# One attention and feed-forward kernel: bias loads after the first pair's loads, scores before tail transposes, another bank for the tail-tail scores

## The chip, the cores and the metric

The kernel runs on one core of a Trainium2 chip. The metric is device microseconds of one execution; lower is better. The engines are named as in the profile: PE (TensorE, matrix products and transposes), ACT (ScalarE), DVE (VectorE), POOL (GpSimd) and SP (SyncE, which only issues transfers). Each engine takes its instructions in the order in which they stand in its own queue, and an instruction that waits holds up everything behind it on that engine.

## The reference, cut to what matters

```python
B, H, S, D = 8, 8, 576, 64                      # q, k, v: [B, H, S, D]
scores = matmul(q, k^T) / sqrt(D) + bias_table[bucket(|i - j|)]   # one bias per head and distance
attn   = exp(scores - max) / sum
x      = (attn @ v)  as [B*S, H*D] = [4608, 512]
out    = ((x @ w_a) * (x @ w_b)) @ w_out        # w_a, w_b: [512, 1536], w_out: [1536, 512]
```

The kernel takes no maximum; it multiplies exp(scores) by exp(bias) instead of adding the bias, and divides by the sum at the end.

## The kernel before, in words

**Pairs.** The 64 heads of all batches are worked through as 32 pairs of heads, p = 0 to 31, four pairs to a batch. Of the 576 positions 512 are the main part (four tiles of 128) and 64 are the tail. For each pair: `qk1(p, t)` makes the scores of key tile t for both heads into a two-bank PSUM buffer of the pool sc (two buffers), `ex(p, t)` takes the Exp of it on ACT (L353), `mul(p, t)` multiplies the band near the diagonal by exp(bias) on DVE (L361). `qk_tail(p)` makes the scores that touch the tail: main keys with tail queries (qkt, L367), tail keys with main queries (qkt, L370) and tail with tail (qktt, L373, into a bank of its own, `pt`); `ex_tail` is their Exp, the small one of qktt first. `av(p, jq)` multiplies by V for query block jq, and `norm(p, 0)` (blocks 0 to 2) and `norm(p, 3)` (blocks 3 and 4) divide by the sum on DVE into XG. `t_x` transposes XG on PE, and `c_x` copies it out of PSUM into `xn_sb`, the input of the feed-forward part. `av_part` is av of pair 3, cut by key tiles.

**Banks.** Apart from sc there are one bank AV (pool `ps_av`), one bank TR (`ps_tr`) and two banks FF (`ps_ff`). Whoever asks for a bank waits until its last reader is done. Q and K of the first three batches are transposed on PE (`t_q`, `t_k` for pair 4 on, `t32`, `q_next`, `k_next` before that) into such a bank, and copied to QT and KT by `c_q`, `c_k`.

**Start.** The head of the kernel (pairs 0 to 3) is written out by hand. The bias table (32 x 8) and a one-hot matrix (oh) are loaded first, on SP's and ACT's queues, then q and k of pair 0 (one head on each of the two queues), then pair 1 and the tails on SP. PE makes five warm-up products on zeros, the product of table and one-hot (L217), three more warm-ups, and then the transposes of k tile 0, of q, and of k tiles 1 to 3 (`t32`, L581). ACT takes the Exp of the product (L220) and stores it to DRAM (`tab`, L221). From there POOL loads the bias windows W0 to W3, one for each pair of heads (`load_w`, L166), and SP the tail window Wt (L225). POOL's queue is: identity, eight cleared tiles, six loads of q, k, v of pairs 2 and 0, W0, two of vt, W1, four of vm, W2, q and k of pair 4, W3, and then the feed-forward weights. SP's queue behind Wt holds the loads of pair 3 (`load32(3, ...)`).

**Transition.** At the end of batch 0 `t_x(0)` to `t_x(2)` take TR, FF, FF; `t_q(4)` and `t_k(4)` take FF, FF; `t_x(3)` takes AV.

**From pair 4 on** each step s is a list of operations with places U in it. At each U some units of the feed-forward part of an earlier batch are put in; a unit is `ff_a` (four products pa and a copy ha on ACT), `ff_b` (four products pb and the multiplication g on DVE) or a third of an output tile (`ff_o`). A step gets a quota of units (12 in step 4, then 7, 6, 4, 4, and 9 from step 9 on), spread evenly over its nine places, so that with fewer than nine some places stay empty. In steps 5 to 10 the step also transposes q and k of pair s + 1, both through the bank TR; qktt of pair s takes TR as well for p < 12.

Of the kernel before, what the change touches and what calls it, by code (L numbers as in the profile page):

```python
# [13 lines left out]
def kernel(  # L14
# [11 lines left out]
    nc = tc.nc  # L26
# [139 lines left out]
        eng.dma_start(out=W_sb[hp][:, :, :],  # L166
                      in_=bass.AP(tensor=tab, offset=2 * hp * TB, ap=[[1, 128], [TB, 2], [1, 384]]))

    nc.sync.dma_start(out=bt_sb[0:NB, :], in_=bias_table)
    nc.scalar.dma_start(out=oh_sb[0:NB, :], in_=oh_handle.ap())  # L170
    make_identity(nc, id32[:, :])
    def pad(eng, x, n):
        eng.memset(x[0:64, :, 1, 0:n], 0.0)
# [6 lines left out]
    def load32(p, src, out, engs):  # L180
        for h in range(2):
            load_h(engs[h], src, out[:, p, :, h, :], 0, 2 * p + h)

    load32(0, q, q32, (nc.sync, nc.scalar))
    load32(0, k, k32, (nc.sync, nc.scalar))
    load32(1, q, q32, (nc.sync, nc.sync))
    load32(1, k, k32, (nc.sync, nc.sync))

# [21 lines left out]
    def warm_up(n):  # L210
        for _ in range(n):
            nc.tensor.matmul(out=warm[:, :], lhsT=zero_sb[:, 0:128], rhs=zero_sb[:, :],
                             start=True, stop=True)

    warm_up(5)
    tps = ps_av.tile([128, 512], FP32, tag="av", name="tab_ps")
    nc.tensor.matmul(out=tps[0:H, 0:NR], lhsT=bt_sb[0:NB, :], rhs=oh_sb[0:NB, :],  # L217
                     start=True, stop=True)
    warm_up(3)
    nc.scalar.activation(out=tab_sb[0:H, 127:127 + NR], in_=tps[0:H, 0:NR], func=ACTF.Exp)  # L220
    nc.scalar.dma_start(out=tab.ap(), in_=tab_sb[0:H, :])  # L221

# [30 lines left out]
    def copy(eng, out, in_):  # L253
        if eng is nc.scalar:
            nc.scalar.activation(out=out, in_=in_, func=ACTF.Copy)
        else:
            nc.vector.tensor_copy(out=out, in_=in_)  # L257
# [21 lines left out]
    def bank(where, dt, name):  # L279
        return where[0].tile([128, 512 if dt is FP32 else 1024], dt, tag=where[1], name=name)  # L280
# [53 lines left out]
    def qk1(p, t, fill=0):  # L334
        qT = qT_(p)
        ps = ps_sc.tile([128, 2, 512], FP32, tag="sc", name=f"qk{p}_{t}")
        for _ in range(fill):
            nc.tensor.matmul(out=ps[:, 0, :], lhsT=zero_sb[:, 0:128], rhs=zero_sb[:, :],
                             start=True, stop=True)
        for hh in range(2):  # L340
            r = slice(64 * hh, 64 * hh + 64)
            nc.tensor.matmul(out=ps[:, hh, :], lhsT=kT_(p, t)[r, :],  # L342
                             rhs=qT[r, :, :], start=True, stop=True)
        st[p]["ps", t] = ps

    def qk(p, t0):
        qk1(p, t0)
        qk1(p, t0 + 1)

    def ex(p, t):  # L350
        ps = st[p]["ps", t]
        at = atp.tile([128, 2, SM], BF16, tag="at", name=f"at{p}_{t}")
        nc.scalar.activation(out=at[:, :, :], in_=ps[:, :, :], func=ACTF.Exp, scale=scale)  # L353
        st[p]["at", t] = at
# [9 lines left out]
    def qk_tail(p):  # L364
        ps = ps_sc.tile([128, 2, 512], FP32, tag="sc", name=f"qkt{p}")
        for t in range(NM):
            nc.tensor.matmul(  # L367
                out=ps[:, 0, :].rearrange("p (h t c) -> p h t c", h=2, t=NM)[:, :, t, :],
                lhsT=kT_(p, t), rhs=qTt_(p), start=True, stop=True)
        nc.tensor.matmul(out=ps[:, 1, :], lhsT=kTt_(p), rhs=qT_(p), start=True, stop=True)  # L370
        pt = bank(TR if p < R3 else AV, FP32, f"qktt{p}")
        for hh in range(2):
            nc.tensor.matmul(out=pt[:, 0:ST], lhsT=kTt_(p), rhs=qTt_(p)[:, ST * hh:ST * hh + ST],  # L373
                             start=(hh == 0), stop=(hh == 1))
        st[p]["ps"] = (ps, pt)
# [204 lines left out]
    def t32(ps, src, p, t):  # L580
        nc.tensor.transpose(ps[:, 128 * t:128 * t + 128], src[:, p, t, :, :], id32[:, :])  # L581

    psk0, psq0 = bank(FF, FP32, "trk0a"), bank(TR, FP32, "trq0a")
    psq1, psk1 = bank(AV, FP32, "trq0b"), bank(FF, FP32, "trk0b")
    t32(psk0, k32, 0, 0)
    for t in range(NM):
        t32(psq0 if t < 2 else psq1, q32, 0, t)
    copy(ACT, QT[0][:, 0:256], psq0[:, 0:256])
    copy(None, KT[0][:, 0:128], psk0[:, 0:128])
    for t in range(1, NM):  # L590
        t32(psk1, k32, 0, t)
    copy(None, QT[0][:, 256:512], psq1[:, 256:512])
    copy(None, KT[0][:, 128:SM], psk1[:, 128:512])
    qk1(0, 0)
    qk1(0, 1, 1)
# [19 lines left out]
    def tails_next(p0, n, eng):  # L615
        ps = bank(FF, FP32, f"trt{p0}")
        for i in range(2 * n):
            nc.tensor.transpose(ps[:, 128 * i:128 * i + 128],
                                (qt32 if i % 2 else kt32)[:, p0 + i // 2, :, :], id32[:, :])
        for i in range(n):  # L620
            copy(eng, KT[(p0 + i) % 2][:, SM:SM + 256], ps[:, 256 * i:256 * i + 256])
# [9 lines left out]
    load32(3, k, k32, (nc.sync, nc.sync))  # L631
    qk1(0, 3)
    ex(0, 2)
    tails_next(0, 2, None)
    qk1(1, 0)
    ex(0, 3)
    ex(1, 0)
    qk_tail(0)
# [5 lines left out]
    for s in (1, 2):  # L644
        if s > 1:
            ex(s, 0)
        mul(s - 1, 3)
        mul_tail(s - 1)
        q_next(s)
        qk1(s, 2)  # L650
        ex(s, 1)
        k_next(s)
        qk1(s, 3)
        ex(s, 2)
        tails_next(s + 1, 1, ACT)
        qk_tail(s)
        mul(s, 0)
        av(s - 1, 0)
        av(s - 1, 1)
        av(s - 1, 2)  # L660
        norm(s - 1, 0)
        mul(s, 1)
        ex(s, 3)
        av(s - 1, 3, FF)
        qk1(s + 1, 0)
        ex_tail(s)
        av(s - 1, 4)
        norm(s - 1, 3)
        mul(s, 2)
        qk1(s + 1, 1)  # L670
# [18 lines left out]
    ex(3, 2)  # L689
    av(2, 3, FF)  # L690
    av(2, 4)
    c_x(1)
    norm(2, 3)
    ex_tail(3)
    qk1(3, 3)
# [2 lines left out]
    t_x(2, FF)  # L698
    mul(3, 1)
    av_part(3, 0)  # L700
    c_x(2, ACT)
    t_q(4, FF)
    c_q(4, ACT)
# [12 lines left out]
    t_x(3, AV, range(3))  # L716
    t_x(3, AV, range(3, 5))
    ff_mm(0, 0, wb_sb, "pb", 0, 3)
    c_x(3)

    def tails4():
        ps = bank(TR, BF16, "trt4")
# [15 lines left out]
    for s in range(4, NP + 1):  # L738
        new = s < NP
        U = "unit"  # L740
        A = lambda *jq: (lambda: [av(s - 1, j, AV if j < 3 or s >= R3 else TR) for j in jq])
        N = lambda j: (lambda: norm(s - 1, j))
        steps = []
        if s == R3:
            ring3 = True
        if s == 4:
            steps += [U, U, lambda: qk1(4, 0), lambda: ex(4, 0), lambda: qk1(4, 1), U, lambda: ex(4, 1),
                      lambda: qk1(4, 2), U, lambda: ex(4, 2), lambda: qk1(4, 3), lambda: ex(4, 3),
                      lambda: mul(4, 0), U, tails4, U, lambda: qk_tail(4), lambda: ex_tail(4),
                      lambda: mul(4, 1), U, lambda: mul(4, 2), U, lambda: mul(4, 3),  # L750
                      lambda: mul_tail(4), U, lambda: t_q(5, TR), lambda: c_q(5), U,
                      lambda: t_k(5, TR), lambda: c_k(5), U, U]
        elif new:
            e = early((s + 1) // 4)
            steps += [lambda: qk(s, 0), lambda: ex(s, 0), U, lambda: ex(s, 1), A(0, 1, 2), N(0), U,
                      lambda: mul(s, 0)]
            av34 = [A(3, 4), N(3)]
            if s - 1 in XD:
                av34 += [lambda: t_x(s - 1), lambda: turns(s)]
            if s < R3:  # L760
                steps += av34
            steps += [U, lambda: mul(s, 1)]
            if s >= R3:
                steps += av34
            steps += [lambda: qk(s, 2), lambda: ex(s, 2)]
            if e:
                steps += [lambda: t_q(s + 1, TR), lambda: c_q(s + 1)]
            steps += [U, lambda: ex(s, 3), U, lambda: mul(s, 2)]
            if e:
                steps += [lambda: t_k(s + 1, TR), lambda: c_k(s + 1)]  # L770
            steps += [U, lambda: mul(s, 3), lambda: qk_tail(s), lambda: ex_tail(s), U]
            if s - 1 not in XD:
                steps += [lambda: t_x(s - 1, TR), lambda: c_x(s - 1), lambda: turns(s)]
            steps += [U, lambda: mul_tail(s), U]
        else:
            steps += [A(0, 1, 2), N(0), U, A(3, 4), N(3), U, lambda: t_x(s - 1, AV),
                      lambda: c_x(s - 1), U, U, U, U, U, U, U]
        quota = quotas.get(s, 9)
        seen, put = 0, 0
        nu = sum(1 for x in steps if x is U)  # L780
        for x in steps:
            if x is U:
                seen += 1
                n = (quota * seen + nu - 1) // nu - put
                put_units(n)
                put += n
            else:
                x()
        b = s // 4 + 1
        if new and s % 4 == 2 and b + 1 < B:  # L790
            load_qkt(b + 1)
        if new and 2 <= b < B:
            if s % 4 == 0:
                load_v(b)
                if b % 2 == 0:
                    load_vt(b, 2)
# [31 lines left out]
```

The softmax here doesn't subtract the row's maximum and nothing guards it: scores larger than these inputs give would overflow.

## Time and profile before

| | |
|---|---|
| median of 8 runs | 418.5 us (418.17 to 418.68) |
| profiled execution, its own time | 418.17 us |
| its span, first to last instruction | 416.4 us |
| granted PE clock, mean | 0.999 |
| PE busy | 403.1 us (97%) |
| ACT busy | 245.3 us (59%) |
| DVE busy | 197.3 us (47%) |
| POOL busy | 119.4 us (29%) |

The profile is of one execution. Times in it count from the first instruction. In a line of the timeline the columns are start and length in us, engine, line of the kernel, operation, what is written from what, its shape, how many were merged, and in brackets how long the engine was idle before it and what ended that. Matrix products overlap with the next ones, so the starts of two products say more than the length of one. A line of the chain has start, length and what it is. A line of the waits has the waiting instruction, what it waited for, the us in total, how often, and the longest.

### The profile page before, as it was taken

Reading aid. Unit: us, or ns where it says so; the run is one execution under the profiler, and the core shown is the slowest. Engines: PE = TensorE matmul, PEld = TensorE weight load, DVE = VectorE, ACT = ScalarE, POOL = GpSimd, SP = SyncE. Lnnn points to the kernel's source line nnn. Section 1 sums busy time; section 2 is a strip of 40 time slices with the busy share of each in tenths; the row PEclk is TensorE's granted clock in tenths of the full one; section 3 lists DMA queues with packets and bytes.
Section 4 is the critical chain, followed back from the end, with each engine's and each line's share of the span. In section 5 each row is a group of like instructions: output and inputs, shape, how many; then the busy total and the mean of one; then the engine's idle time right before and its main releaser. Section 6 shows DMA issues by size and latency. Waiting matters only on the chain.

```text
span 416.4 us, 8424 instructions
## 1 busy us (share of the span) xinstructions
PE 403.1 (97%) x3350; PEld 207.5 (50%) x3407; DVE 197.3 (47%) x485; ACT 245.3 (59%) x345; POOL 119.4 (29%) x161
## 2 busy tenths in 40 slices
PE   8799999999999999999999999999999999999996
PEld 3573555555454555544554455555545554444443
DVE  4585666556542555255525553455425540430430
ACT  4887566756656766577666665666567642322321
POOL 9898839904428000920073003000000000000000
PEclk9999999999999999999999999999999999999999
DMA  9999999999949950999099919921120002002004
GB/s 160 191 162 171 159 171 150 177 147 105 124 60 171 177 44 17 169 185 96 16 117 194 120 20 75 174 51 39 41 90 5 12 17 101 2 0 102 2 0 101
DMA packets 164935, 40.75 MB, mean 98 GB/s; under 512 B 155320, under 2 KB 160224, under 8 KB 164896
## 3 DMA queue, kind: packets, MB, share of 16 engines
q0 software_dynamic: 110448, 18.75, 63.2%
q1 hardware_dynamic: 53168, 21.03, 27.7%
q10 hardware_dynamic: 1280, 0.43, 0.5%
q8 instruction: 26, 0.43, 0.4%
q14 instruction: 13, 0.11, 0.1%
HBM read 38.77 MB, written 9.45 MB: 116 GB/s over the span
## 4 chain that ended last, share of the span: by engine, by line
PE 91%; DVE 3%; POOL 2%; issue 1%; DMA 1%; ACT 1%; DVEq 0%; POOLq 0%; ACTq 0%
PE pb L511 22%; PE pa L511 22%; PE po L542 22%; PE av L412 9%; PE qk L342 7%; PE av L403 2%; PE qkt L367 1%; PE qkt L370 1%; DMA W<-bias_tab 1%; DVE at L361 1%; PE qktt L373 1%; PE trx L475 1%; PE po L530 1%; DVE KT L257 1%; DVE XG L449 1%
## 5 line engine op out<-in xcount | busy, mean ns | idle before, releaser
L353 ACT ACTIVATE at<-qk 128x1024 bf16<-128x1024 f32 x128 | 126.2, 1023 | 24.7 <-PE qk L342 24.7
L523 DVE TENSOR_TENSOR g<-pb,ha 128x512 bf16<-128x512 f32 x108 | 74.7, 691 | 118.2 <-PE pb L511 105.1
L511 PE MATMUL pa<-xn,wa 128*128 128x512 bf16 x417 | 110.1, 380 | 1.1 <-issue 0.3
L511 PE MATMUL pb<-xn,wb 128*128 128x512 bf16 x411 | 109.1, 379 | 1.1 <-issue 0.2
L518 ACT ACTIVATE ha<-pa 128x512 f32<-128x512 f32 x108 | 64.6, 598 | 66.7 <-PE pa L511 66.1
L542 PE MATMUL po<-wo,g 128*128 128x512 bf16 x403 | 96.3, 380 | 1.1 <-issue 0.3
L511 PEld LDWEIGHTS <-wa 128*128 128x128 bf16 x432 | 39.3, 98 | 49.7 <-issue 8.8
L361 DVE TENSOR_TENSOR at<-at,W 128x512 bf16<-128x512 bf16 (+1 forms) x128 | 59.0, 483 | 8.4 <-ACT at L353 5.5
L511 PEld LDWEIGHTS <-wb 128*128 128x128 bf16 x432 | 39.4, 98 | 46.8 <-issue 5.9
L542 PEld LDWEIGHTS <-g 128*128 128x128 bf16 x420 | 37.9, 98 | 46.3 <-issue 7.4
L123 POOL DMA_DIRECT2D vm<-in_v_dram x32 | 28.2, 919 | 102.2 <-PE av L412 61.9
L546 ACT ACTIVATE ob<-po 128x512 f32<-128x512 f32 x35 | 20.9, 597 | 60.7 <-PE po L542 58.7
L412 PE MATMUL av<-vm,at 128*128 128x65 bf16 x992 | 43.3, 193 | 0.0
L412 PEld LDWEIGHTS <-at 128*128 128x128 bf16 x992 | 39.4, 97 | 6.2
L448 DVE RECIPROCAL rc<-av 128x6 f32<-128x6 f32 x64 | 12.0, 187 | 53.8 <-PE av L412 52.1
L403 PE MATMUL av<-vt,att 128*128 128x130 bf16 x156 | 34.7, 222 | 0.0
L381 ACT ACTIVATE att<-qkt 128x1024 bf16<-128x1024 f32 x32 | 32.7, 1020 | 0.0
L449 DVE TENSOR_TENSOR XG<-av,rc 128x384 bf16<-128x384 f32 x64 | 31.4, 491 | 2.4 <-DVE rc L448 0.2
L123 POOL DMA_DIRECT2D qn<-in_q_dram x28 | 24.4, 919 | 24.2 <-PE trq L291 16.9
L123 POOL DMA_DIRECT2D kn<-in_k_dram x28 | 24.5, 916 | 4.1 <-DMA vt<-in_v_dram 1.9
L342 PE MATMUL qk<-QTb,KTb 64*128 64x512 bf16 x160 | 24.2, 381 | 0.0
L403 PEld LDWEIGHTS <-att 128*128 128x128 bf16 x156 | 15.3, 98 | 7.4 <-issue 0.7
(121 smaller groups left out, 239.9 us busy)
## 6 DMA issues: line engine op xcount, KB each, us to landing
out_dram<-ob SPq DMA_DIRECT2D x32, 256.0 KB, 4.3
vm<-in_v_dram POOLq DMA_DIRECT2D x28, 128.0 KB, 5.4
qn<-in_q_dram POOLq DMA_DIRECT2D x24, 128.0 KB, 7.8
kn<-in_k_dram POOLq DMA_DIRECT2D x24, 128.0 KB, 9.6
wa<-in_moe_w_a_dram POOLq DMA_DIRECT2D x3, 512.0 KB, 6.8
wb<-in_moe_w_b_dram POOLq DMA_DIRECT2D x3, 512.0 KB, 10.0
wo<-in_moe_w_out_dram POOLq DMA_DIRECT2D x1, 1536.0 KB, 13.1
W<-bias_tab POOLq DMA_DIRECT2D x4, 192.0 KB, 5.5
```

The source lines that it names most:

```text
L123: nc.gpsimd.dma_start(out=(vm[b % 2][:, h0:h1, t, 0:Dh] if dst is None else dst[b % 2][:, :].rearrange("p (t h d) -> p t h d", h=H, t=NM)[ ...
L342: nc.tensor.matmul(out=ps[:, hh, :], lhsT=kT_(p, t)[r, :], rhs=qT[r, :, :], start=True, stop=True)
L353: nc.scalar.activation(out=at[:, :, :], in_=ps[:, :, :], func=ACTF.Exp, scale=scale)
L361: nc.vector.tensor_tensor(out=at[:, :, lo:hi], in0=at[:, :, lo:hi], in1=w[:, :, y:(None if z < 0 else z):-1], op=MULT)
L381: nc.scalar.activation(out=at[:, 0:1024].rearrange("p (a x) -> p a x", a=2), in_=ps[:, :, :], func=ACTF.Exp, scale=scale)
L403: nc.tensor.matmul(out=pav[:, slot, :, :], lhsT=x, rhs=vt[b // 2 % 2][:, 4 * i + hp, :, 0:Dh + 1], start=fresh, stop=True, skip_group_chec ...
L412: nc.tensor.matmul(out=pav[:, slot, hh, :], lhsT=x, rhs=vm[i][:, 2 * hp + hh, t, 0:Dh + 1], start=False, stop=True, skip_group_check=True)
L449: nc.vector.tensor_tensor(out=xg[:, j0:j0 + n, :, :], in0=pav[:, 0:n, :, 0:Dh], in1=rc.unsqueeze(3).to_broadcast([128, n, 2, Dh]), op=MULT)
L511: nc.tensor.matmul(out=ff[key][:, :], lhsT=w[df // FW][:, mc, 128 * (df % FW):128 * (df % FW) + 128], rhs=xn_sb[mc][:, xin(c)], start=(i = ...
L518: nc.scalar.activation(out=ha[:, :], in_=ff["pa"][:, :], func=ACTF.Copy)
L523: nc.vector.tensor_tensor(out=g_sb[df][:, :], in0=ff["pb"][:, :], in1=ff["ha"][:, :], op=MULT)
L542: nc.tensor.matmul(out=po[:, :], lhsT=g_sb[df][:, 128 * tt:128 * tt + 128], rhs=wo_sb[:, df, :], start=(df == 0), stop=(df == NDF - 1))
```

## The change

1. The loads of the bias table and of the one-hot matrix stand behind the loads of q and k of pair 0 on SP's and ACT's queues.
2. Seven warm-ups ahead of the table product and one behind it, instead of five and three. The transposes of pair 0 run q first, then all of k; KT's first 128 columns are copied by ACT instead of DVE.
3. `qk1(1, 0)` stands ahead of `tails_next(0, 2)` on PE.
4. `tails_next(s + 1, 1)` in s = 1, 2 copies on DVE instead of ACT.
5. qktt takes the bank AV instead of TR for pairs 4 to 11.
6. `c_x(1)` moves from DVE (between av and norm of pair 2) to ACT, behind the Exp of pair 3's last tile and just ahead of `c_x(2)`. The copy `c_x(3)` is split: 384 columns on ACT, 128 and the 64 of the tail on DVE.
7. In the steps from pair 5 on, the place U that stood behind `t_q`, `c_q` of the next pair stands ahead of them. PE's order changes by this in steps 5, 6, 9 and 10; in steps 7 and 8 that place is empty.

```diff
-    nc.sync.dma_start(out=bt_sb[0:NB, :], in_=bias_table)
-    nc.scalar.dma_start(out=oh_sb[0:NB, :], in_=oh_handle.ap())
...
     load32(0, q, q32, (nc.sync, nc.scalar))
     load32(0, k, k32, (nc.sync, nc.scalar))
+    nc.sync.dma_start(out=bt_sb[0:NB, :], in_=bias_table)
+    nc.scalar.dma_start(out=oh_sb[0:NB, :], in_=oh_handle.ap())
...
-    warm_up(5)
+    warm_up(7)
     tps = ps_av.tile([128, 512], FP32, tag="av", name="tab_ps")
     nc.tensor.matmul(out=tps[0:H, 0:NR], lhsT=bt_sb[0:NB, :], rhs=oh_sb[0:NB, :],
                      start=True, stop=True)
-    warm_up(3)
+    warm_up(1)
...
-        pt = bank(TR if p < R3 else AV, FP32, f"qktt{p}")
+        pt = bank(TR if p < 4 else AV, FP32, f"qktt{p}")
...
-    t32(psk0, k32, 0, 0)
     for t in range(NM):
         t32(psq0 if t < 2 else psq1, q32, 0, t)
+    for t in range(NM):
+        t32(psk1 if t else psk0, k32, 0, t)
     copy(ACT, QT[0][:, 0:256], psq0[:, 0:256])
-    copy(None, KT[0][:, 0:128], psk0[:, 0:128])
-    for t in range(1, NM):
-        t32(psk1, k32, 0, t)
     copy(None, QT[0][:, 256:512], psq1[:, 256:512])
+    copy(ACT, KT[0][:, 0:128], psk0[:, 0:128])
     copy(None, KT[0][:, 128:SM], psk1[:, 128:512])
...
     ex(0, 2)
+    qk1(1, 0)
     tails_next(0, 2, None)
-    qk1(1, 0)
     ex(0, 3)
...
-        tails_next(s + 1, 1, ACT)
+        tails_next(s + 1, 1, None)
...
     av(2, 4)
-    c_x(1)
     norm(2, 3)
...
     av_part(3, 0)
+    c_x(1, ACT)
     c_x(2, ACT)
...
-    c_x(3)
+    copy(ACT, xn_sb[3][:, 0:384], st[3]["x"][:, 0:384])
+    copy(None, xn_sb[3][:, 384:SM], st[3]["x"][:, 384:SM])
+    copy(None, xn_sb[3][:, xc(0)[1]], st[3]["x"][:, SM:S])
...
-            steps += [lambda: qk(s, 2), lambda: ex(s, 2)]
+            steps += [lambda: qk(s, 2), lambda: ex(s, 2), U]
             if e:
                 steps += [lambda: t_q(s + 1, TR), lambda: c_q(s + 1)]
-            steps += [U, lambda: ex(s, 3), U, lambda: mul(s, 2)]
+            steps += [lambda: ex(s, 3), U, lambda: mul(s, 2)]
```

## The prediction

> **What bounds the kernel now.** I read the page first: TensorE (PE) is busy 403.1 of 416.4 us, so from about 34 us on a microsecond is won only where PE itself waits, and lost wherever a new wait stands in its queue. Then the busy times by stretch, to see where PE isn't full.
>
> ```profile
> 18.00:28.00 10.00, 9.86 (x157) 6.88 (x155) 9.27 (x30) 9.08 (x13) 8.99 (x16) 1.00 1.39 159
> ```
>
> The columns are stretch, length, then busy us of PE, weight loads, VectorE (DVE), ScalarE (ACT), GpSimd (POOL). Between 18 and 28 us DVE (9.27) and ACT (9.08) are nearly full too; from 34 to 104 PE is busy 67.81 of 70, ACT 46.50 and DVE 42.00. Next the chain of waits in the first 36 us:
>
> ```profile
> 8.03 1.42 POOL vm L129 x2
> 9.44 4.81 DMA W<-bias_tab
> ...
> 16.35 0.35 DVE QT L257
> 16.70 0.04 issue
> 16.74 0.22 PE qktt L373 x2
> ```
>
> The chain comes down POOL's queue (qn, kn, vm from 4.95 on, W0's issue at 9.44) and passes through the landing of W0, the first bias window. The multiplications of pair 0 (L361) wait for it; behind them in DVE's queue stands the copy of pair 2's QT, and that frees the bank for pair 1's qktt on PE. The timeline says how each engine stands to it:
>
> ```profile
> 4.90 0.79 ACTq L221 DMA_DIRECT2D bias_tab<-tab_sb  x1
> 6.17 0.38 ACT L255 ACTIVATE QT<-trq0a 128x256 bf16<-128x256 f32 x1 [1.29 <-PE trq0a L581]
> ...
> 12.04 1.02 ACT L353 ACTIVATE at<-qk 128x1024 bf16<-128x1024 f32 x1 [0.97 <-PE qk L342]
> ...
> 14.35 1.70 DVE L361 TENSOR_TENSOR at<-at,W 128x512 bf16<-128x512 bf16 x4 [1.89 <-DMA W<-bias_tab]
> ```
>
> DVE idles 1.89 us for W0, longer than any wait of ACT between 7.3 and 34. Last, PE's waits between 46 and 104 us:
>
> ```profile
> PE qktt L373 <- DVE KT L257: 1.0, 4, 0.4
> PE trq L291 <- DVE XG L449: 0.2, 1, 0.2
> ```
>
> **Part 1, bias loads behind q and k of pair 0.** The one-hot load (oh) goes from first to third on ACT's queue: its issue moves from 0.75 to 0.75+0.54+0.53 = 1.82. If it takes 1.8 us to land as before, it is there at 3.6; if it stays behind k on the same queue, it lands after k, which took 3.6 us from its issue at 1.77 and is now issued 0.48 earlier: 4.9. I take 4.9, because two loads of 128 KB stand before it on its queue and the loads landed in the order of issue (oh 2.58, q 4.09, k 5.40).
>
> *A rule against the change: the Trainium skill, "DMA: Bandwidth & Descriptors", section "Queues, rings and completion order", says that each DMA engine takes a queue's descriptors in ring order. By it oh can't pass k and 4.9 holds; without it 3.6 is open. The landings above agree.*
>
> PE's queue has the table product (L217) ahead of all transposes, in both kernels. It started at 3.44 after the fifth warm-up; now it waits until 4.9, 1.46 later. It is followed by the Exp (4.50 to 4.87) and the store of the table (4.90), whose landing released SyncE's Wt load at 8.64; with 1.46 added that is 10.1. POOL reaches its W0 issue at 9.44 and now waits there until 10.1: 0.66 late, with vt, W1, vm, W2, the weights behind it. (Ends: oh at 3.6 costs nothing, the table landing at 8.8; oh at 5.0 costs 0.8.) Is the 0.66 hidden in the transfer queue? The 128-byte packets of the six loads before W0 have all begun by 11.75, and W0's first packet began at 11.61, 2.17 after its issue, like qn's first (4.90 to 7.00, 2.1). W0 was not queued, so the delay passes. W1 was queued behind vt (6.6 us to landing against 4.8), so a part may be absorbed: 0 to 0.66. DVE starts pair 1 with W1's landing and is then full until 28, so W1's delay is what reaches 28 us. I take **+0.6** (0 to +0.8). On SyncE's queue Wt waits 1.46 longer and the loads of pair 3 behind it go from 10.43 to about 11.6; they landed at 16.9 (q) and 18.6 (k), would land near 18.1 and 19.8, and are read at 19.20 and 20.10: hidden, with 0.3 to spare for k.
>
> **Part 2, first transposes, pair 1's scores early.** The ScalarE queue issues the table's store for 0.79 us. That was hidden (4.90 to 5.69, before QT's copy at 6.17). Now Exp runs 5.96 to 6.33, the issue to 7.15, QT's copy to 7.53, KT's copy (128 columns, new on ACT; between 0.26 for 64 columns and 0.38 for 256) to 7.80, the first score and its 0.43 to the Exp: 8.27 instead of 7.30. Four Exps later pair 1's first stands at 8.27 + 4 x 0.94 = 12.03; in the trace it is at 12.04 after its 0.97 idle, which the reordering removes. So the two cancel. The tails' transposes, which waited for their load until 11.03, now stand behind that score: 11.4 to 11.85, DVE's copy to 12.3, qkt and qktt to 13.0, so ex_tail starts at 13.05 instead of 12.96. The 0.1 is hidden by W0: ACT's ex_tail of pair 1 waits for qktt, and so for W0, anyway.
>
> **Part 3, tail copies from ACT to DVE (pairs 2, 3).** ACT loses 2 x 0.28. DVE gains 2 x 0.34: the first falls in DVE's 0.94 us wait for W1, the second in its 0.35 wait for av at 23.08. At nothing; 0.34 each if that cover goes, and no gain from ACT, which waits for PE again at 27.1 (0.48).
>
> **Part 4, end of batch 0.**
>
> ```profile
> 28.12 1.03 ACT L353 ACTIVATE at<-qk 128x1024 bf16<-128x1024 f32 x1
> 29.02 0.73 ACT L255 ACTIVATE xn<-trx 128x512 bf16<-128x512 bf16 x2
> ...
> 29.06 0.39 PE L291 MATMUL trq<-cst_sb,qn 128*128 128x128 bf16 x4
> ```
>
> c_x(1) leaves DVE, where it ran 27.30 to 27.81 and ended as DVE had to wait for av anyway (0.01 gained), and stands on ACT after ex(3,3). Its bank trx1 is one of two; trx2 takes the other, so t_q(4) on PE now waits for c_x(1): as c_x(2) did, it would end at 29.75, and PE resumes at 29.80 instead of 29.06. Queued behind it: av_part of pair 3, norm, t_x(3), the first feed-forward product. PE is dense there, so **+0.74**; zero only if ACT ran 0.74 ahead of PE, which ex_tail(3) waiting for PE denies. The split of c_x(3) replaces a DVE copy of 0.42 by an ACT copy of 384 columns: between 0.38 (256) and 0.62 (512), 0.50 by proportion, **+0.08**.
>
> **Part 5, qktt in the value bank, unit before t_q.** A step without waiting starts 0.216 after the 512-column product; in pairs 5 to 9 it starts 0.583, 0.589, 0.588, 0.588 and 0.526 after. Together 1.79 lost; the value bank was read long before, so **-1.79**. The moved unit has a price. In pair 5 (7 units for 9 places) nothing is left between t_q and t_k, which share one bank, and the DVE copy between them now stands behind a g multiplication.
>
> ```profile
> 50.86 1.03 PE L511 MATMUL pb<-xn,wb 128*128 128x512 bf16 x4
> 51.06 0.42 DVE L257 COPY QT<-trq 128x512 bf16<-128x512 bf16 x1 [0.23 <-PE trq L291]
> ...
> 51.72 0.39 PE L311 MATMUL trk<-cst_sb,kn 128*128 128x128 bf16 x4
> ...
> 51.99 0.69 DVE L523 TENSOR_TENSOR g<-pb,ha 128x512 bf16<-128x512 f32 x1 [0.51 <-PE pb L511]
> ```
>
> pb moves up 0.23, g starts at 51.76, the QT copy 0.61 later at 52.37 and ends at 52.79; trk at 52.83 instead of 51.72: **+1.11**. Pairs 6 and 10 have one unit between (0.86); the same sum gives a wait of 0.23 each. Pair 6 drops its 0.27 wait for XG (**-0.04**); pair 10 pays **+0.23**. Pair 9's unit before is pa, with no g: nothing; pairs 7, 8 have no unit there.
>
> **Sum.** 0.6 + 0 + 0.74 + 0.08 - 1.79 + 1.11 - 0.04 + 0.23 = +0.93. The profiled execution took 418.17 (span 416.4 and 1.8 around it), the lowest of the eight; the median is 418.5. On it: **419.4**.
>
> **The clock.** The warm-ups stand 0.43 us apart; from 5.64 the 128-column transposes stand 0.11 apart, and the granted clock's record begins at 5.62, after 4.4 us of nearly unbroken work. Now seven warm-ups end at 1.20 + 7 x 0.43 = 4.2 and PE is idle until 4.9. If it stays slow for the eight transposes, that is 0.87 on ACT's start; W0's 0.66 and ACT's 0.28 cover it. If it stays slow until 14, PE's 6.15 busy us of 6 to 14 nearly double: some +2.
>
> *The Trainium skill, "TensorE: Matmul & The Clock Gate", "Part 1: The HAM clock gate", asks for one busy window of about 3.4 us. Seven warm-ups fill 3.0: by the rule the clock would rise later than in the trace and the +2 would be due; no run here shows it yet.*
>
> **Rivals.** (A) W0's delay is absorbed: oh lands early or the transfers catch up. For it: DMA is idle a part of 12 to 14 us (73 to 176 GB/s). Sum 0.33: 418.8. (B) Faster: ACT, not W0, sets the head. Then the 0.28s count and c_x(1) is done before PE asks: 0.08 - 0.49 - 0.56 = -0.97: 417.5. It decides if W0 lands by 14.3 and DVE doesn't wait for it; against it stands the 1.89 idle. (C) The slow clock: +0.93 + 2 = 421.4.
>
> **How the numbers follow.** Forecast 0.55, with 418.6 to 419.8 as its own range (head 0 to 0.8, part 4 0.6 to 0.9); A 0.18, B 0.12, C 0.15. What a measurement can tell from no change is 0.2%, 0.84 us, so the forecast lies just over that: of its 0.55 I give 0.35 to slower and 0.20 to same; of A 0.04 and 0.14. Slower 0.35 + 0.04 + 0.15 = 0.54, same 0.34, faster 0.12. The range leaves out B and the upper part of C: 418.2 to 420.7.
>
> **What would show it.** Right: the table product starts near 4.9, W0's issue near 10.1, DVE's wait for W0 is longer than 1.89; trq of pair 4 waits for ACT's xn copy; no qktt wait after 46 us; one wait of about 1.1 us of trk for the QT copy near 53. Wrong: W0 landing at 14.3 or before, trq of pair 4 not waiting, or transposes 0.21 apart after 6 us.

## The result and the profile after

The changed kernel takes 420.61 us in the median of 11 runs (419.03 to 421.58); the kernel before took 418.48 in the 31 runs beside them (417.9 to 420.13). The ratio is 1.0047 with a 95% interval of 1.0037 to 1.0057: slower by 2.0 us (1.5 to 2.4), where +0.93 was forecast. The profiled execution took 420.32, its span 418.5 against 416.4.

The span says at once where to look. Three places cut it into parts that can be compared between the two traces: the start of the Exp of pair 3's last tile, the start of pair 4's first Exp, and the end of the last instruction.

| part of the span, us | before | after | difference | forecast |
|---|---|---|---|---|
| head, to the last Exp of pair 3 | 28.12 | 29.65 | +1.53 | +0.60 |
| transition, to pair 4's first Exp | 5.83 | 6.78 | +0.95 | +0.82 |
| the rest, to the end | 379.11 | 378.75 | -0.36 | -0.49 |
| sum | 413.06 | 415.18 | +2.12 | +0.93 |

(The span ends some 3.3 us after the last compute instruction in both.) Two of the three parts came out within 0.13 us of the forecast. The head did not. (How far it is off, one profile says only roughly: in the five profiles of kernels whose code is the same up to this Exp, the kernel before and four of the runs below, the head takes between 28.12 and 29.04 us, and the kernel before has the shortest.) Here is the chain of waits of the changed kernel there (start, length, what it was):

```profile
1.90 3.68 DMA oh_sb<-oh
5.62 0.59 PE tab_ps L217 x2
...
7.85 0.61 PE qk L342 x2
8.46 0.54 PE qk L338
9.00 0.54 PE qk L342 x2
9.54 1.05 PE trq L581 x4
...
11.91 0.69 DVE KT L257
12.66 0.39 PE qk L342 x2
13.04 0.60 PE trt L617 x4
13.67 0.43 DVE KT L257
```

Before, this chain came down POOL's queue to W0's landing. Now W0 is not on it. It starts with the landing of the one-hot matrix at 5.58 (forecast 4.9), goes through PE's products, which between 8 and 10.5 us stand 0.54 apart (0.32 in the kernel before), and then through the K copy that pair 1's first scores wait for and the tails' transposes behind them. The wait is in PE's list, one line for each sort of wait (us in total, times, longest):

```profile
PE tab_ps L217 <- DMA oh_sb<-oh: 1.4, 1, 1.4
```

The busy times by stretch show why the products stood so far apart. The columns are as before: PE, weight loads, DVE, ACT, POOL, then PE's granted clock, the DMA share and GB/s.

```profile
4.20:5.70 1.50, 0.11 (x2) 0.08 (x2) 0.00 (x0) 0.00 (x0) 1.46 (x3) 1.00 1.36 209
5.70:7.40 1.70, 1.70 (x11) 0.94 (x10) 0.24 (x1) 0.53 (x2) 1.70 (x4) 0.99 1.24 166
7.40:10.80 3.40, 3.16 (x12) 1.17 (x10) 0.92 (x3) 2.44 (x4) 3.16 (x5) 0.50 1.81 156
```

PE is busy 0.11 of the 1.50 us in which it waits for oh. From 7.4 to 10.8 the clock is at half, 0.50, and PE is then busy 3.16 us for 12 instructions; before, the same stretch had a clock of 1.00 and 16 instructions in 2.58 us:

```profile
7.40:10.80 3.40, 2.58 (x16) 1.19 (x15) 1.39 (x4) 3.40 (x4) 3.40 (x6) 1.00 2.34 160
```

So ACT gets its scores late. First the kernel before, then the changed one:

```profile
7.30 3.77 ACT L353 ACTIVATE at<-qk 128x1024 bf16<-128x1024 f32 x4 [0.75 <-PE qk L342]
...
12.96 0.22 ACT L380 ACTIVATE att<-qktt 128x64 bf16<-128x64 f32 x1
```

```profile
8.50 2.10 ACT L353 ACTIVATE at<-qk 128x1024 bf16<-128x1024 f32 x2 [0.70 <-PE qk L342]
11.32 2.86 ACT L353 ACTIVATE at<-qk 128x1024 bf16<-128x1024 f32 x3 [0.72 <-PE qk L342]
14.86 0.22 ACT L380 ACTIVATE att<-qktt 128x64 bf16<-128x64 f32 x1 [0.68 <-PE qktt L373]
```

The first Exp stands at 8.50 (before 7.30, forecast 8.27), but the Exp of pair 0's tails at 14.86 (before 12.96, forecast 13.05). Most of the half-clock stretch lies between the two.

At the transition, PE's list has the new wait that was forecast, and ACT's and DVE's timelines have one that was not:

```profile
PE trq L291 <- ACT xn L255: 0.4, 1, 0.4
```

```profile
30.55 1.34 ACT L255 ACTIVATE xn<-trx 128x512 bf16<-128x512 bf16 x4
...
34.68 0.49 ACT L255 ACTIVATE xn<-trx 128x384 bf16<-128x384 bf16 x1 [0.83 <-PE trx L475]
```

```profile
35.20 0.32 DVE L257 COPY xn<-trx 128x128 bf16<-128x128 bf16 x2 [0.90 <-ACT xn L255]
```

The ACT part of the split copy `c_x(3)` runs from 34.68 to 35.17, and the DVE part, meant to run beside it, starts at 35.20 and names the ACT copy as what it waited for. Further on, PE's waits between 46 and 106 us are one line, where the kernel before had the four of qktt:

```profile
PE trk L311 <- DVE QT L257: 1.0, 1, 1.0
```

### The profile page after: what moved, and what is told of

Same layout as the page of the kernel before. It is cut to its first block, busy times and chain, and to the rows that moved or that the text cites. A ratio compares the mean times of both kernels' runs of the same rounds, so it can differ in the third digit from the quotient of the medians.

```text
span 418.5 us, 8427 instructions
## 1 busy us (share of the span) xinstructions
PE 403.7 (96%) x3350; PEld 207.8 (50%) x3407; DVE 197.2 (47%) x484; ACT 246.0 (59%) x347; POOL 119.4 (29%) x161
## 4 chain that ended last, share of the span: by engine, by line
PE 93%; ACT 2%; DVE 2%; issue 1%; DMA 1%; ACTq 0%; DVEq 0%
PE pa L511 22%; PE pb L511 22%; PE po L542 22%; PE av L412 9%; PE qk L342 8%; PE av L403 2%; PE qkt L367 2%; PE qkt L370 1%; ACT at L353 1%; DMA oh_sb<-oh 1%; PE po L530 1%; PE trx L475 1%; PE qktt L373 1%; PE trk L311 0%; DVE g L523 0%
```

## The experiments

A ratio stands against runs of the kernel before on the same chip (medians 418.49 to 418.63), with its 95% interval; 0.1% is 0.42 us. Theory 1: the late one-hot load, through PE's queue and the clock, makes the loss of the head. Theory 2, that of the forecast: the bias window W0 is late. Theory 3: the new order of scores and tails does it.

**The bias loads alone.** The kernel before, with

```diff
-    nc.sync.dma_start(out=bt_sb[0:NB, :], in_=bias_table)
-    nc.scalar.dma_start(out=oh_sb[0:NB, :], in_=oh_handle.ap())
...
     load32(0, k, k32, (nc.sync, nc.scalar))
+    nc.sync.dma_start(out=bt_sb[0:NB, :], in_=bias_table)
+    nc.scalar.dma_start(out=oh_sb[0:NB, :], in_=oh_handle.ap())
...
-    warm_up(5)
+    warm_up(7)
...
-    warm_up(3)
+    warm_up(1)
```

> The kernel before with the two bias loads alone put behind the first pair, and the warm-ups 7 and 1. Theory 1 (the table product, ahead of the transposes in PE's queue, waits for oh_sb, and the clock falls to half after that idle stretch): oh_sb lands near 5.6, the first transposes start near 6.3, the clock is at half for one stretch of 3.4 us, the exponential of the tails of pair 0 is 1.0 to 1.6 later than 12.96, and the total is 1.0 to 1.6 us above the kernel before. Theory 2 (the tables W are late, as forecast): the clock stays full after 7 us, W0 lands 0.2 to 0.6 later, the multiplications wait for it, total +0.2 to +0.6. Theory 3 (the order of scores and tails makes the loss): the loads alone cost under 0.3.

Measured: 420.13 us, ratio 1.0030 (1.0017 to 1.0043), so +1.3 (0.7 to 1.8). The table product starts at 5.58, the first transposes at 6.33, the Exp of pair 0's tails at 14.05 (+1.09), and the clock record has half speed from 7.66 to 11.07:

```profile
7.40:10.80 3.40, 3.16 (x13) 1.28 (x12) 0.98 (x3) 2.23 (x3) 2.98 (x5) 0.54 1.90 164
```

```profile
15.24 1.70 DVE L361 TENSOR_TENSOR at<-at,W 128x512 bf16<-128x512 bf16 x4 [1.68 <-ACT att L381]
```

W0 landed at 15.14 here (before 14.26). DVE's multiplications ended their wait at 15.21 with ACT, 0.07 after W0. So theory 1 holds for the total and for where the clock falls, theory 3 is not needed, and theory 2 is not refuted: in this execution both came together. The head of this profile, which is of the fastest of the twelve executions, takes 29.01 us; two profiles further down that load the bias first take 29.04 and 29.01, with W0 landing at 15.17 and 15.15. The loss is seen in the medians, not in this trace.

**The bias loads put back.** The changed kernel with the loads first again and `warm_up(5)`, `warm_up(3)`.

> The changed kernel with the bias loads first again and the warm-ups 5 and 3; all else stays changed. Theory 1: oh_sb lands near 2.6, no half-clock stretch after 7 us, 1.0 to 1.6 us below the changed kernel, so 419.0 to 419.6. Theory 2: 0.2 to 0.6 below it. Theory 3 (order): within 0.3 of the changed kernel.

Measured: 419.14, ratio 1.0011 (1.0002 to 1.0021). Against the changed kernel's 1.0047 that is 1.5 us less, the gain that theory 1 named. The clock is full from 4.99, and the first Exp starts at 6.87, earlier than before the change. But DVE waits longer for W0 than in either kernel:

```profile
15.20 1.70 DVE L361 TENSOR_TENSOR at<-at,W 128x512 bf16<-128x512 bf16 x4 [2.74 <-DMA W<-bias_tab]
```

W0 was issued at 9.44 as in the kernel before and landed at 15.10 instead of 14.26. Theory 3 is out as a cause by itself: all of the new order is still in this kernel. Whether the order adds to late loads was not tried; with the clock falling, the tails' Exp stands at 14.86 with it (the changed kernel) and at 14.05 without it (the bias loads alone).

**More warm-ups.** The changed kernel with

```diff
-    warm_up(7)
+    warm_up(13)
```

> The changed kernel with 13 warm-up products ahead of the table product in place of 7: PE is busy until about 5.6, when oh_sb lands, so nothing real starts later. If the half-clock stretch of 7.4 to 10.8 us comes from the idle stretch before the table product and carries most of the loss: full clock after 4 us, transposes of trq1 0.11 apart in place of 0.21, the exponential of pair 0's tails 0.6 to 1.0 earlier, total 0.6 to 1.0 below the changed kernel. If the late oh_sb alone carries it: 0 to 0.2 below.

Measured: 419.81, ratio 1.0025 (1.0017 to 1.0034): 0.9 us below the changed kernel, though oh lands just as late (5.69) and the first Exp starts at 8.38. The stretch that was at half clock:

```profile
7.40:10.80 3.40, 3.11 (x21) 1.41 (x19) 1.56 (x4) 2.91 (x5) 3.04 (x5) 1.00 1.77 152
```

It has 21 instructions of PE in 3.11 us, against 12 in 3.16. The Exps follow each other without a gap from 8.38 to 13.07, and the tails' Exp starts at 13.73, 1.13 earlier. Busy zeros in place of the idle stretch are worth 0.9 us. The other 0.6 of the 1.5 remains (the intervals of this run and of the loads put back just overlap). In this profile W0 was issued 0.43 later than before and landed at 15.29, DVE waited 2.1 us for it, and pair 2's first Exp started 4.3 us after the landing, as it did before (18.58 after 14.26). (The chain of this profile names the tail window, which DVE needs next and which landed at 15.83; the 4.3 us speak for W0.) That is the forecast's mechanism, but it is one profile.

The fall of the clock is not in every execution. The mean clock of the profiles that have it is 0.994 (the changed kernel) and 0.996 (the bias loads alone). Of the changed kernel's twelve executions six have 0.994 or 0.995 and took 420.32 to 420.90; the other six have 0.998 to 1.000 and took 419.03 to 421.58, so they are not faster. Of the twelve with the bias loads alone two have 0.996, and they are the two fastest. The mean doesn't count the time before the record of full clock begins (it is 0.999 for a profile below in which PE runs at half until 10.33), and the heads of these executions were not kept, so what PE's clock was there is not shown. With 13 warm-ups all eleven have 0.999 or 1.000 and lie between 419.54 and 420.14. What the run shows, then, is that the idle stretch costs 0.9; that it does so through the fall at 7.4 us is seen in one trace, and whether a later rise of the clock does it elsewhere is not shown.

**The order alone.** The kernel before with

```diff
-    tails_next(0, 2, None)
     qk1(1, 0)
+    tails_next(0, 2, None)
```

> The kernel before with the scores of pair 1, tile 0, put ahead of the tails' transposes, and nothing else. Theory 3: the scores wait on PE for pair 1's K copy with the tails' transposes behind them, so the exponential of pair 0's tails comes 0.3 to 0.6 later and the total rises by as much. Theory 1 (and the forecast): the idle 0.97 us of ScalarE ahead of pair 1's first exponential gets shorter, the tails are no later, total 0 to -0.9.

Measured: 418.53, ratio 0.9997 (0.9989 to 1.0006). The idle time goes (Exps at 10.88 and 11.79 in a row), the tails' Exp comes at 13.50 instead of 12.96, and neither reaches the end. (The 0.54 is not the order's: full clock begins at 7.87 in this profile, 5.62 in the kernel before, and already the first Exp stands at 8.14 instead of 7.30.) The forecast's 0 holds.

**`c_x(1)` on ACT alone.** The kernel before with

```diff
-    c_x(1)
...
+    c_x(1, ACT)
     c_x(2, ACT)
```

> The kernel before with the copy of pair 1's output alone moved to ScalarE, behind the last exponential of pair 3. By the forecast's term the transposes of pair 4's queries wait for that copy's bank: trq of pair 4 starts 0.7 later, and the total rises by 0.74. If the earlier DVE work pays it back (norm and multiplications of pair 2 and 3 start 0.6 earlier), the total rises by less than 0.3.

Measured: 419.07, ratio 1.0015 (1.0003 to 1.0026), +0.6. In its timeline of PE:

```profile
29.92 0.38 PE L291 MATMUL trq<-cst_sb,qn 128*128 128x128 bf16 x4 [0.44 <-ACT xn L255]
```

The last Exp of pair 3 is at 28.23 here, so trq starts 1.69 after it, where it was 0.94: +0.75, against the +0.74 forecast. Up to pair 4's first Exp 0.63 of it is left (6.46 against 5.83).

**The split copy, in one bank and in two.** The first is the kernel before with the split of the change; in the second, transposes 3 and 4 go to the bank TR, and DVE copies from there:

```diff
-    t_x(3, AV, range(3, 5))
+    x3b = bank(TR, BF16, "trx3b")
+    for jq in range(3, 5):
+        nc.tensor.transpose(x3b[:, 128 * jq:128 * jq + 128], XG[3][:, jq, :, :], ident)
...
-    c_x(3)
+    copy(ACT, xn_sb[3][:, 0:384], st[3]["x"][:, 0:384])
+    copy(None, xn_sb[3][:, 384:SM], x3b[:, 384:SM])
+    copy(None, xn_sb[3][:, xc(0)[1]], x3b[:, SM:S])
```

> The kernel before with the last output copy of batch 0 alone split, 384 columns on ScalarE and 128 on DVE. The forecast: the two run side by side, the product pa starts 0.08 later, total +0.1 at most. The reading of the changed kernel's trace: the DVE copy starts only after the ScalarE copy has ended, pa starts 0.3 later, total +0.2 to +0.4.

> The same split, but the last two of the five transposes go to a second PSUM bank (that of the transposes), so that the two engines read different banks. If the DVE copy waited because both read one bank: here it runs beside the ScalarE copy, pa starts 0.0 to 0.1 later than in the kernel before, total within 0.15 of it. If it waited because both write one SBUF tile: it still starts after the ScalarE copy, total +0.2 to +0.4.

Measured: 419.01, ratio 1.0008 (0.9997 to 1.0020), for one bank; 418.68, ratio 1.0000 (0.9990 to 1.0009), for two. The intervals overlap, but the timelines don't leave it open. One bank, ACT and then DVE:

```profile
32.94 0.49 ACT L255 ACTIVATE xn<-trx 128x384 bf16<-128x384 bf16 x1 [0.84 <-PE trx L475]
```

```profile
33.46 0.22 DVE L257 COPY xn<-trx 128x128 bf16<-128x128 bf16 x1 [0.90 <-ACT xn L255]
```

Two banks:

```profile
32.35 0.49 ACT L255 ACTIVATE xn<-trx 128x384 bf16<-128x384 bf16 x1 [0.34 <-PE trx L475]
```

```profile
32.84 0.32 DVE L257 COPY xn<-trx3b 128x128 bf16<-128x128 bf16 x2 [0.38 <-PE trx3b L719]
```

With one bank DVE's copy waits for ACT's; with two it waits only for its own transposes, which end at 32.80 (ACT's copy starts earlier too, ahead of them, and happens to end at 32.84, so these two runs alone show no overlap). Both copies write one SBUF tile in both kernels, and that doesn't keep them apart: in the changed kernel's start DVE copies into QT from 7.16 to 7.58 and ACT from 7.24 to 7.62, out of two banks. So the wait belongs to the common bank, not to the common tile. From pair 3's last Exp to pair 4's first it is 6.14 us with one bank, 5.79 with two, and 5.83 without the split: the split in one bank costs 0.31, in two it brings nothing that counts.

**The value bank for qktt alone.** The kernel before with

```diff
-        pt = bank(TR if p < R3 else AV, FP32, f"qktt{p}")
+        pt = bank(TR if p < 4 else AV, FP32, f"qktt{p}")
```

> The kernel before with the tail-tail scores of pairs 4 to 11 alone in the value bank. The forecast's term: PE's waits ahead of qktt in pairs 5 to 9 go, 1.79 us less. Rival: what PE no longer waits for here it waits for at the next score or value bank, and the total falls by under 0.6.

Measured: 417.57, ratio 0.9971 (0.9961 to 0.9982): 1.2 us faster (0.8 to 1.6), and faster than both kernels. Between 46 and 104 us PE's only wait is the old one of pair 6:

```profile
PE trq L291 <- DVE XG L449: 0.2, 1, 0.2
```

From pair 4's first Exp to the end the trace has 377.60 us against 379.11, 1.51 less. Steps 5, 6, 8 and 9 give 0.30 to 0.37 each, step 7 only 0.16. There PE's last transpose of pair 8's keys waits 0.2 us for its load, which landed at 71.84 (the transpose starts at 71.89).

**The same with the moved unit.** As above, and

```diff
-            steps += [lambda: qk(s, 2), lambda: ex(s, 2)]
+            steps += [lambda: qk(s, 2), lambda: ex(s, 2), U]
...
-            steps += [U, lambda: ex(s, 3), U, lambda: mul(s, 2)]
+            steps += [lambda: ex(s, 3), U, lambda: mul(s, 2)]
```

> The kernel before with the tail-tail scores in the value bank and the unit of work moved ahead of the query transposes, both and nothing else. The forecast's terms: against the kernel with the tail-tail scores alone, PE's key transposes of pair 5's step wait 1.0 to 1.1 for the QT copy again, total +0.6 to +1.1 against it, so 418.1 to 418.6. Rival: the moved unit also takes waits of later steps away, total within 0.3 of that kernel.

Measured: 418.31, ratio 0.9989 (0.9976 to 1.0003), 0.75 more than without the unit's move (the intervals overlap; in the traces it is 1.15). Its waits between 46 and 106 us are the line of trk for QT (1.0) that the changed kernel has. Step 5 takes 11.46 us instead of 10.34, which is +1.12; step 10 takes +0.26; step 7 takes 0.21 less, since the load that the last run waited for has landed in time here.

**W0 and W1 on SP's queue.** The kernel before with

```diff
-    load_w(nc.gpsimd, 0)
+    load_w(nc.sync, 0)
     for hh in range(2):
         nc.sync.dma_start(out=Wt_sb[...
+    load_w(nc.sync, 1)
     load_vt(0, 1)
-    load_w(nc.gpsimd, 1)
```

> The kernel before with the loads of W0 and W1 on SP's queue, ahead of Wt's, in place of POOL's. If W0's landing sets the head of the kernel before (DVE's 1.89 us of waiting for W): W0 lands before 13.5, DVE no longer waits for it, pair 2's first exponential starts 0.3 to 0.8 before 18.58, total 0.3 to 0.8 less. If the landing is hidden anyway: total within 0.2 of the kernel before.

Measured: 419.18, ratio 1.0015 (0.9999 to 1.0030), a miss. (In this edit W0's load stands ahead of Wt's, W1's behind it.) The first half of the expectation came true: W0 landed at 12.81, DVE waited 0.2 us for W in all. Yet pair 2's first Exp moved only from 18.58 to 18.47, since ACT was next. And the loads of pair 3 on the same queue now stood behind W1, as the chain shows:

```profile
12.82 8.26 DMA k<-in_k_dram
21.08 0.14 issue
21.22 0.63 PE trk L581 x4
```

Pair 3's k landed at 21.08 instead of 18.61, and pair 2's last Exp, whose scores stand behind that transpose on PE, came 1.1 later (22.85 against 21.77), pair 3's first with it (24.77 against 23.71). This wait took the place of W0's.

**All that looked good together** (value bank for qktt, the order of scores and tails, W0 and W1 on SP).

> The kernel before with three things: the tail-tail scores of pairs 4 to 11 in the value bank, pair 1's first scores ahead of the tails' transposes, and W0 and W1 on SP's queue. If the terms add up: -1.2 from the first, 0 to -0.5 from the second, 0 to -0.8 from the third, so 416.2 to 417.4 and faster than both kernels. If W0's landing is hidden anyway, the first alone remains: 417.2 to 417.6.

Measured: 417.71, ratio 0.9975 (0.9962 to 0.9989). Faster than both kernels, but no better than the value bank alone. Its profile has pair 3's late loads too (pair 2's last Exp at 22.58, before 21.77).

**Late bias loads without their two suspected costs.** The kernel before with the loads behind the first pair, 13 and 1 warm-ups, and W0 and W1 on SP.

> The kernel before with the bias loads behind the first pair, 13 warm-ups ahead of the table product and 1 behind it, and W0 and W1 on SP's queue: neither the half-clock stretch nor W0's landing on POOL's queue is left, only that oh_sb comes late. Against the kernel before with W0 and W1 on SP's queue alone: if the clock and W0 carry the whole loss of the late bias loads, within 0.3 of it; if the late first transposes carry a part of their own, 0.4 to 0.8 above it.

Measured: 423.20, ratio 1.0113 (1.0085 to 1.0140), outside both expectations, and no answer to the question. In its profile the clock was not full until 6.93, so the 13 warm-ups took until 6.8 and held the table product to 6.86, though oh had landed at 5.62. The table was then stored late, W0 landed at 15.11 and the tail window at 18.27, and pair 3's k at 24.64, so pair 2's last Exp stood at 26.41. What the late first transposes cost by themselves stays open.

## Why the prediction was right or wrong

The direction was right; the size was half of what came. The 420.61 lies inside the range, but 0.09 below its upper end and outside the 418.6 to 419.8 that the forecast had for itself: that the range holds it is owed to rival C, which was counted in. That the transition and the rest came out within 0.13 is partly luck too: in each, two terms were off in ways that cancel (the table). Each term beside its runs (us; the runs are ratios times 418.5):

| term | forecast | run that isolates it | in the traces |
|---|---|---|---|
| part 1, bias loads | +0.6 | +1.3 alone; -1.5 undone | +1.53 (whole head, against the shortest of five) |
| part 2, order | 0 | -0.1 | with the above |
| part 3, tail copies on DVE | 0 | not tried alone | 0 (9.54 from pair 2's first Exp to pair 3's last, in both) |
| part 4, `c_x(1)` | +0.74 | +0.6 | +0.63 |
| part 4, split | +0.08 | +0.3 | +0.31 |
| part 5, qktt | -1.79 | -1.2 | -1.51 |
| part 5, unit | +1.30 | +0.75 | +1.15 |
| sum | +0.93 | +1.7 | +2.1 |

The runs add up to 1.7 with part 1 done alone, against 2.0 (1.5 to 2.4) measured for the change.

**The step that failed is part 1.** Three things in it. First, the landing: oh was to land right behind k of its queue, at 4.9; k landed near 5.0, but oh another 0.6 later, at 5.58. Second, the path: the delay was followed through the table to W0, and there the forecast was too high. The table product ran at full clock (0.59 instead of 1.02), the store took 2.81 us from its issue to its landing instead of 3.74 and landed at 9.46 instead of the 10.1 that I had, W0 was issued at 9.74 instead of 10.1. Third, and largest, the paragraph on the clock asked the right question and took the wrong end. It priced "slow for the eight transposes" (0.87, covered by W0) and "slow until 14" (+2, rival C). What came in the profile was a third case: full clock when the warm-ups ended, so the eight transposes ran fast, then half clock for one stretch of 3.41 us, 7.37 to 10.78, under the first scores. With busy warm-ups in place of the idle stretch 0.9 us came back; the 0.6 left of part 1's 1.5 is the size that was forecast, but which of W0, the late first scores and the order makes it stays open. Rival C, at 421.4, had the mechanism, and it came at about half the price that I had put on it.

The marks set for "wrong" say the same: transposes did stand 0.21 apart after 6 us (9.47 to 10.3), and W0 at 14.45 landed 0.15 above the mark while DVE did not wait for it (its work before ended at 14.43). Rival B had such a point: ACT, not W0, would set the head. It did, but with ACT late through PE, not with the 0.28s saved. That the forecast's own mechanism, W0, is right behind is seen in the profile of the warm-up run, where DVE waits 2.1 us for it again. Rival A fell with the bias loads alone at +1.3.

The Trainium skill, "TensorE: Matmul & The Clock Gate", "HAM oscillation", states the rule as no idle gaps of PE above some 3.4 us. In this trace the clock fell after less: the full-clock stretch lasted 3.41 us, PE was idle for 1.4 of it, and the next stretch was at half. The measurement decides against the rule, but gives none in its place. With qktt alone in the value bank PE waits longer at one go, 1.53 us up to 11.58 for a load, and the clock stays full:

```profile
3.95:7.37 3.42, 2.03 (x12) 1.03 (x11) 0.21 (x1) 0.50 (x2) 3.38 (x6) 1.00 1.29 189
```

```profile
8.73:12.15 3.42, 1.89 (x13) 1.05 (x12) 1.25 (x4) 2.41 (x3) 3.42 (x7) 1.00 1.97 180
```

The first line is the changed kernel ahead of the fall, the second that run around its wait; PE is busy 2.03 and 1.89 of 3.42 us. The two falls on record both follow the first 3.41 us of full clock; why they came there stays open. The one busy window of about 3.4 us, which the prediction took from the same page, was not needed either: the record of full clock begins at 3.95, 2.75 us after the first warm-up.

**The split** was the second mis-sized term: I put the two copies side by side and they ran one after the other, +0.3 for +0.08. The Trainium skill says so in "PSUM — Partial Sum Buffer", section "PSUM bank collisions raise a hardware error": two engines must not read one bank and quadrant at a time, so a program has to put a wait between them. I had not weighed it. The runs with one and two banks agree: DVE starts 0.03 after ACT's end in the one, and waits for PE alone in the other.

**Right as worked out:** the wait of trq for `c_x(1)` (+0.75 at trq, +0.74 forecast), the wait of trk for the QT copy (step 5: +1.12, forecast +1.11), step 10 (+0.25, forecast +0.23), no qktt wait left after 46 us, and the order of scores and tails, by itself, at nothing. qktt gave 1.51 in the trace instead of 1.79; 0.2 of the difference is step 7, where PE waited for the load of pair 8's keys, and with the unit moved, where that load was in time, it was back.

## What to carry to other kernels

A load that feeds a product at the front of an in-order queue holds everything behind it, however small it is: follow a delay first through the queue in which the waiting instruction stands, and only then down the data. Before filling an idle stretch or opening one near the start, ask what the clock does with it; and before cutting a copy in two for two engines, see that the halves lie in different banks. Of the seven edits here one was shown to be worth keeping: the one that moved waiting products into a bank that had long been read.

## What the runs showed of the hardware

The clock fell back to half for one stretch of 3.41 us in two profiles, after 3.41 us of full clock in which PE had been idle for 1.39 us at one go (the changed kernel) and 1.20 us (the bias loads alone). The length of the gap does not decide by itself: gaps of 1.53 us (qktt alone) and 1.59 us (the last run, up to 19.17) later on left the clock full. Half speed alone did not make a head as long as the changed kernel's: in the profile of the split in one bank PE ran at half until 10.33, and its head took 28.55 us, 0.43 more than in the kernel before and 1.10 less than in the changed one. Where the record of full clock begins is not the kernel's alone: in the ten profiles that load the bias first and make five warm-ups ahead of the table product it begins between 5.0 and 10.3 us, and PE runs at half speed until then.

The landing of one and the same load varies more than most edits here are worth. W0, issued on POOL's queue at 9.44 to 9.46 us in eight profiles (the kernel before, the loads put back, the order alone, `c_x(1)`, the two splits, the two of the value bank), landed between 13.66 and 15.17. In the six of them in which the landing came at 14.2 or later, pair 2's first Exp started 4.31 or 4.32 us after it; so a single profile of the head says little below a microsecond, and the medians had to decide.
